# A convolution moved to channels on the partitions, and its logits from eight matmul tiles to four

## The chip, the cores and the metric

The kernel runs on one core of a Trainium2 chip. The metric is the device time of one execution in microseconds (us). The kernel before took 1312.17 us, the median of three runs (1308.29 to 1316.62).

## The reference

A depthwise causal convolution over 8 sequences of 3584 tokens with 192 channels comes first; the 7 taps are a softmax per head, and a head is 24 neighbouring channels. Then each token goes to one of 8 experts. The chosen expert can be inherited from the token before, so routing is a scan along the sequence.

```python
# convolution: x (8, 3584, 192), weight (8 heads, 7 taps)
w = softmax(weight, axis=-1)
out[b, s, h*24:(h+1)*24] = sum(w[h, k] * x_pad[b, s + k, h*24:(h+1)*24] for k in range(7))
# mixture of experts on that output, called x again
logits = x @ w_gate                      # (8, 3584, 8)
local_gate = sigmoid(x @ w_local)
for b in range(B):
    prev_e = -1
    for s in range(S):
        fresh_e = argmax(logits[b, s])
        e = fresh_e if s == 0 or local_gate[b, s] < 0.5 else prev_e
        prev_e = e
        p = softmax(logits[b, s])
        out[b, s] = p[e] * (relu(x[b, s] @ w1[e]) @ w2[e])     # w1: 192x1024, w2: 1024x192
```

All numbers are float32.

## The kernel before, in words

The 28672 tokens form 16 groups of 1792 (14 tokens on each of 128 partitions). Groups 0 and 1 take another way, with the convolution on TensorE (`wide`), and the change touches little of it. Each of the groups 2 to 15 goes through the following steps.

1. `conv` (L402): the window of x, 20 rows of 192 channels per partition, lies in `x_sb` with tokens on the partitions. For each of the 8 heads ScalarE writes the first tap (L413, 128x336 elements in 14 runs of 24) and VectorE adds the six others (L423), 48 VectorE instructions a group. The result is written straight into the group's token rows `y_sb`, which also hold the gate's factor and the token number.
2. `logits` (L601): VectorE turns the rows in 32x32 blocks into `z` (L606, four instructions), so that channels lie on the partitions, with four sets of 32 partitions for four sets of tokens. TensorE multiplies z by the gate's weights (L620): per block of 32 channels four column places times two row halves of 64 partitions. ScalarE copies the result out of PSUM (L625), VectorE turns it back (L628), and 16 small copies per group (L642 on ScalarE or L644 on VectorE) put it in order.
3. `route` (L650): argmax, the scan of inherited experts, and each token's place in its expert's list, some fifty small VectorE instructions; then tables of full units (`table`).
4. `put` (L821): GpSimd scatters the rows, 128 tokens at a time, into `slots` in DRAM, 14 times a group (L828).

Experts work on blocks of 128-token units of one expert, in this order: 28 single blocks, 43 pair blocks, then 23 blocks of four and a tail. A single or pair block is: rows loaded (L978), turned by TensorE (L394), hidden layer (L1047), relu on ScalarE (L1056), output layer (L1068), scaling of one half of the sum on ScalarE (L1078), and of the other, added to it, on VectorE (L1082), which frees the PSUM of the product, then a scatter into the output (L1096). Blocks of four multiply with seven products in place of eight (`seven`, L1211 to L1246; L1217 is the copy of its first product) and end with L1261, L1271 and L1276.

The order of instructions is written out by the program itself; each engine works through its own queue in that order. Between the parts of a block `step(time)` (L1322) emits side work, convolution and routing, until costs of `time` are used up. The costs are numbers that the generators yield: 0.6 for a tap, 0.2 for most small instructions. A pair block has steps of 4.8, 1.2 and 3.6, a single block 2.1, 1.2 and 1.3, a block of four the four of `SIDE`. A step runs until its time is zero or less; outside the blocks of four what it overshoots is forgotten. Routing comes first where it can run; at "pe" it waits for a step with room in PSUM, at "hop" it yields to convolution for the rest of the step.

Four pools of one buffer (`ys`) hold the token rows of four, later three groups; `yt` holds z. Convolution of group g starts only when the scatters of group g - 3 have been emitted and routing of group g - 2 has begun (L1297). From the last pair blocks on, the fourth pool holds the rows of blocks of four.

The softmaxed taps `c` are made at the start on one partition and spread to all by a matmul that also spreads the sums' reciprocals `rz` (L211 to L216). `rz` and the exponentials `hank` serve groups 0 and 1.

Of the kernel before, what the change touches and what calls it, by code (L numbers as in the profile page):

```python
# [8 lines left out]
F32 = mybir.dt.float32  # L9
# [86 lines left out]
TQ = (NT + 3) // 4  # L96
WA = F * KD // 2
# [14 lines left out]
def kernel(  # L112
# [4 lines left out]
    weight: bass.AP,  # L117
    wh: bass.AP,
# [28 lines left out]
    def load_x(g):  # L147
        x_sb = xs.tile([P, NX, D], F32, name="x_sb")
        src = x[g // PER]
        win = bass.AP(tensor=src.tensor, offset=src.offset + g % PER * PT * D,  # L150
                      ap=[[NT * D, P], [1, NX * D]])
        nc.sync.dma_start(out=x_sb.rearrange("p t d -> p (t d)"), in_=win)
        return x_sb
# [14 lines left out]
    c = cst.tile([P, H, KC], F32, name="c")  # L168
    nm = cst.tile([P, H], F32, name="nm")
    rz = cst.tile([P, H], F32, name="rz")  # L170
    with tc.tile_pool(name="scr", bufs=1) as scr:
# [6 lines left out]
        nc.sync.dma_start(out=wg, in_=wgl)  # L178
        x_in[1] = load_b(1)
# [13 lines left out]
        wide_w = scr.tile([P, 2 * H + H * KC], F32, name="wide_w")  # L193
# [9 lines left out]
        wc = ws[:, H:].rearrange("o (h k) -> o h k", k=KC)  # L203
# [7 lines left out]
        nc.vector.tensor_tensor(wc, w, bcast(ws[:, :H], KC), op=Alu.mult)  # L211
        cps = hps_p.tile([P, 512], F32, name="hps")
        nc.tensor.matmul(cps[:, :H + H * KC], lhsT=ones, rhs=wide_w[:, H:], start=True, stop=True)
        awake(2)
        nc.vector.tensor_copy(rz, cps[:, :H])
        nc.vector.tensor_copy(c.rearrange("p h k -> p (h k)"), cps[:, H:H + H * KC])  # L216
    wgb, wgq = wg[:, :3, :], wg[:, 3:, :]

# [179 lines left out]
    def row_tile(g):  # L398
        at = g % 4 if g < NARROW else (g + 1) % 3
        return ys[at].tile([P, NB, DG], F32, name="y_sb")  # L400

    def conv(g, x_sb):  # L402
        y_sb = row_tile(g)[:, :NT, :]
        got[g] = y_sb

        def cols(h):
            return y_sb[:, :, Y0 + h * GS:Y0 + (h + 1) * GS]

        def chans(h, k):
            return x_sb[:, k:k + NT, h * GS:(h + 1) * GS]  # L410

        def first(h):
            nc.scalar.activation(cols(h), chans(h, 0), Act.Copy, scale=c[:, h, 0:1])  # L413

        first(0)
        yield 0
        for h in range(H):
            if h + 1 < H:
                first(h + 1)
            if h == H // 2 and 2 < g < NPART - 1:  # L420
                x_in[g + 1] = load_x(g + 1)
            for k in range(1, KC):
                nc.vector.scalar_tensor_tensor(cols(h), chans(h, k), c[:, h, k:k + 1],  # L423
                                               cols(h), Alu.mult, Alu.add)
                yield 0.6
# [175 lines left out]
    def logits(g, y_sb):  # L601

        z = z_tile()[:, :NT * D].rearrange("p (t d) -> p t d", d=D)
        for t in range(0, NT, TQ):
            u = min(t + TQ, NT)
            nc.vector.transpose(z[:, t:u, :], y_sb[:, t:u, Y0:Y0 + D])  # L606
            yield 0.2 * (u - t)
        yield "pe"


        if late_p:
            both = st["bank"].tile([P, 2, 512], F32, name="ps")
            lps = [both[:, half, :TQ * Q] for half in range(2)]
        else:
            lps = [hps_p.tile([P, TQ * Q], F32, name="hps") for half in range(2)]
        begin = [min(TQ * j, NT - TQ) for j in range(4)]
        for b in range(DQ):
            for j in range(4):
                for half, rows in halves():
                    nc.tensor.matmul(lps[half][Q * j:Q * j + Q, :], lhsT=wgq[rows, b, :],  # L620
                                     rhs=z[rows, begin[j]:begin[j] + TQ, b * Q:(b + 1) * Q],
                                     start=(b == 0), stop=(b == DQ - 1))
# [4 lines left out]
        lq = sm.tile([P, 2 * TQ, Q], F32, name="lq", bufs=1)  # L627
        nc.vector.transpose(lq.rearrange("p t e -> p (t e)"), ls.rearrange("p h x -> p (h x)"))  # L628
        yield 0.4
        lt = sm.tile([P, NT + 2, E + 1], F32, name="lt")  # L630
# [3 lines left out]
        for r in range(4):  # L634
            for j in range(4):
                t, u = TQ * j, min(TQ * (j + 1), NT)
                at = r // 2 * TQ + t - begin[j]
                e0 = r % 2 * (E + 1)
                dst = lt[Q * r:Q * r + Q, t:u, :]
                src = lq[Q * j:Q * j + Q, at:at + u - t, e0:e0 + E + 1]  # L640
                if aside:
                    nc.scalar.copy(dst, src)  # L642
                else:
                    nc.vector.tensor_copy(dst, src)  # L644
                    yield 0.12
            if aside:
                yield "hop"
        return lt

    def route(g):  # L650
        y_sb = got.pop(g)
        lt = yield from logits(g, y_sb)
        lg = lt[:, :NT, :E]
# [15 lines left out]
        nc.vector.tensor_scalar(fr, lt[:, :NT, E], 0.0, None, Alu.is_lt)  # L669
# [579 lines left out]
    def output_late(n, wb, xg, hT, rows_next=None, between=None):  # L1249

        for part, h in enumerate(hT):
# [35 lines left out]
    LEAD = 2  # L1287
# [3 lines left out]
          "due": False, "hot": False, "since": 0, "bank": None, "over": 0}  # L1291

    def start_conv():
        g = st["conv"] + 1

        free = not any(p[0] <= g - 3 for p in to_put)
# [303 lines left out]
```

## Time and profile before

| what | value |
|---|---|
| median of three runs | 1312.17 us |
| profiled execution: time, span | 1309.78 us, 1308.1 us |
| mean granted TensorE clock | 0.998 |
| TensorE, VectorE, ScalarE, GpSimd busy | 98%, 73%, 47%, 42% of the span |
| taps on VectorE (L423) | 672, 384.5 us |
| logits on TensorE (L620) | 1344 matmul records, 25.0 us |

The profile is of one execution. A row of a group gives the line, engine, operation, tiles and shapes, the count, then busy time and the mean duration in ns, then the engine's idle time ahead of it and what ended it. A matmul of float32 numbers shows as two records. A row of the order of time begins with start and length in us and can hold several instructions (x16); idle time before it and its releaser stand in brackets. PE is TensorE, PEld its weight loads, DVE VectorE, ACT ScalarE, POOL GpSimd; ends of matmuls are modelled, so a busy TensorE can hide small gaps.

### The profile page before, as it was taken

How to read it: one execution, taken by the hardware profiler on the slowest of the kernel's cores; microseconds unless marked ns; L12 is line 12 of the kernel's file. 1: busy time of each engine (PE TensorE's matmuls, PEld its weight loads, DVE VectorE, ACT ScalarE, POOL GpSimd, SP SyncE). 2: the span in 40 equal slices, each digit the busy share in tenths (PEclk: the TensorE clock that was granted, in tenths of full speed). 3: DMA queues.
4: the chain of work that ended last, by engine and by line, in shares of the span. 5: the costliest groups of instructions: out<-in, count | busy, mean ns of one | idle time of the engine just before them, and what ended most of it. 6: DMA issues, size and time to landing. Idle time of an engine off the chain costs nothing. (4 is left out here: it accounts for less than half of the span.)

```text
span 1308.1 us, 39979 instructions
## 1 busy us (share of the span) xinstructions
PE 1276.2 (98%) x15750; PEld 1206.7 (92%) x15750; DVE 956.1 (73%) x2602; ACT 617.5 (47%) x1407; POOL 553.1 (42%) x619
## 2 busy tenths in 40 slices
PE   9899999999999999999999999999999999999997
PEld 7798999999999999899999899999999899999996
DVE  5888898889888788788988998898857844431111
ACT  5345555445555645456463454454434434342332
POOL 4444443534344444444435633654462664421211
PEclk9999999999999999999999999999999999999999
DMA  5789988857767767667696655555455637536894
GB/s 197 272 342 387 373 345 347 296 201 270 259 213 263 257 219 259 215 231 259 206 282 174 181 163 154 149 150 151 125 171 113 194 108 189 155 95 193 268 326 156
DMA packets 130243, 291.18 MB, mean 223 GB/s; under 512 B 87936, under 2 KB 104759, under 8 KB 114306
## 3 DMA queue, kind: packets, MB, share of 16 engines
q1 hardware_dynamic: 107728, 243.35, 56.6%
q0 software_dynamic: 22320, 45.22, 10.2%
q8 instruction: 126, 2.06, 0.7%
q14 instruction: 67, 0.55, 0.1%
q10 hardware_dynamic: 2, 0.00, 0.0%
HBM read 242.92 MB, written 46.07 MB: 221 GB/s over the span
## 5 line engine op out<-in xcount | busy, mean ns | idle before, releaser
L423 DVE SCALAR_TENSOR_TENSOR y_sb<-x_sb,c,y_sb 128x336 f32<-128x336 f32 x672 | 384.5, 581 | 33.3 <-ACT y_sb L413 11.0
L1068 PE MATMUL yps<-wb,hT 64*128 64x192 f32 x3648 | 318.6, 326 | 5.2 <-ACT hT L1056 3.0
L1047 PE MATMUL hps<-xT,wb 64*128 64x256 f32 (+1 forms) x3408 | 315.4, 336 | 2.6 <-issue 1.3
L828 POOL DMA_INDIRECT slots<-y_sb,posi x228 | 227.9, 1000 | 208.9 <-PE yps L1068 150.3
L1261 PE MATMUL ps<-wb,hot 64*128 64x192 f32 x3680 | 309.7, 324 | 2.1 <-issue 1.8
L1261 PEld LDWEIGHTS ps<-wb,hot 64*128 64x128 f32 x3680 | 299.3, 187 | 9.4 <-ACT hot L1235 5.0
L1068 PEld LDWEIGHTS yps<-wb,hT 64*128 64x128 f32 x3648 | 297.4, 187 | 10.2 <-ACT hT L1056 5.1
L1047 PEld LDWEIGHTS hps<-xT,wb 64*128 64x128 f32 x3408 | 283.2, 187 | 23.6 <-issue 3.6
L1096 POOL DMA_INDIRECT out_dram<-o_sb,head x115 | 120.6, 1049 | 296.7 <-DVE o_sb L1276 270.9
L1056 ACT ACTIVATE hT<-hps 128x512 f32<-128x512 f32 (+1 forms) x284 | 130.4, 510 | 161.0 <-PE hps L1047 116.5
L1096 POOL DMA_INDIRECT out_dram<-o_sb,xg x114 | 117.1, 1028 | 207.8 <-DVE o_sb L1082 112.4
L1271 ACT ACTIVATE o_sb<-ps,head 128x192 f32<-128x192 f32 x115 | 43.0, 418 | 205.2 <-PE ps L1261 178.9
L1276 DVE SCALAR_TENSOR_TENSOR o_sb<-ps,head,o_sb 128x192 f32<-128x192 f32 x115 | 43.2, 411 | 111.2 <-ACT o_sb L1271 108.6
L1029 ACT COPY xT<-xps 64x256 f32<-64x256 f32 (+4 forms) x284 | 105.1, 370 | 9.5 <-PE yps L1068 2.2
L1078 ACT ACTIVATE o_sb<-yps,xg 128x192 f32<-128x192 f32 x114 | 43.3, 418 | 125.2 <-PE yps L1068 96.9
L1135 DVE STREAM_TRANSPOSE xT<-y_sb 128x768 f32<-128x768 f32 (+1 forms) x65 | 54.8, 870 | 61.7 <-PE ps L1156 31.2
L1211 PE MATMUL ps<-xT,wb 64*128 64x256 f32 x736 | 88.5, 377 | 1.0 <-DVE xT L1187 1.0
L1211 PEld LDWEIGHTS ps<-xT,wb 64*128 64x128 f32 x736 | 75.3, 187 | 4.9 <-issue 2.2
L1082 DVE SCALAR_TENSOR_TENSOR o_sb<-yps,xg,o_sb 128x192 f32<-128x192 f32 x114 | 43.4, 412 | 33.1 <-ACT o_sb L1078 27.5
L1235 ACT ACTIVATE hot<-hot 128x512 f32<-128x512 f32 x46 | 26.4, 622 | 83.6 <-DVE hot L1233 61.1
L1156 PE MATMUL ps<-xT,wb 64*128 64x128 f32 (+1 forms) x912 | 64.5, 294 | 0.5 <-DVE xT L1135 0.5
L1156 PEld LDWEIGHTS ps<-xT,wb 64*128 64x128 f32 x912 | 62.6, 188 | 1.2 <-DVE xT L1135 1.1
(281 smaller groups left out, 1337.8 us busy)
## 6 DMA issues: line engine op xcount, KB each, us to landing
wb<-in_w_dram SPq DMA_DIRECT2D x109, 1536.0 KB
x_sb<-in_x_dram SPq DMA_DIRECT2D x14, 1920.0 KB
y_sb<-slots SPq DMA_DIRECT2D x92, 192.0 KB
xg<-slots SPq DMA_DIRECT2D x43, 195.0 KB
wb<-in_w_dram SPq DMA_DIRECT2D x12, 512.0 KB
slots<-y_sb,posi POOLq DMA_INDIRECT x228
x_sb<-in_xb_dram SPq DMA_DIRECT2D x4, 768.0 KB
y_sb<-slots SPq DMA_DIRECT2D x60, 48.0 KB
```

The lines of the kernel that those rows point to most:

```text
L423: nc.vector.scalar_tensor_tensor(cols(h), chans(h, k), c[:, h, k:k + 1], cols(h), Alu.mult, Alu.add)
L828: ins = nc.gpsimd.indirect_dma_start(out=slots[:, :], in_=rows, in_offset=None, out_offset=bass.IndirectOffsetOnAxis(ap=to, axis=0)).ins
L1029: copied = nc.scalar.copy(a, b)
L1047: ins = nc.tensor.matmul(hps[half][:, j, w], lhsT=wb[rows, f0:f0 + P], rhs=xT[rows, d, w], start=(d == 0 and j == 0), stop=(d == KD - 1), ...
L1056: nc.scalar.activation(hT[:, m:m + 2, w], hps[half][:, :, w], Act.Relu)
L1068: ins = nc.tensor.matmul(yps[half][:, k * D:(k + 1) * D], lhsT=hT[rows, m, k * P:(k + 1) * P], rhs=wb[rows, WA + m * D:WA + (m + 1) * D], ...
L1082: nc.vector.scalar_tensor_tensor(o_sb[:, k, :], y[k][1], xg[:, k, 0:1], o_sb[:, k, :], Alu.mult, Alu.add)
L1096: sent = nc.gpsimd.indirect_dma_start(out=out, in_=o, in_offset=None, out_offset=bass.IndirectOffsetOnAxis(ap=xg.bitcast(I32)[:, k, 1:2], ...
L1135: nc.vector.transpose(xT.rearrange("p d (j t) -> p j d t", t=Q)[:, js], rows[:, js].rearrange("p j (d t) -> p j d t", t=Q))
L1156: nc.tensor.matmul(hps[:, half, j, :], lhsT=wb[rows, f0:f0 + P], rhs=xT[rows, d, :], start=(d == 0 and j == 0), stop=(d == KD - 1), skip_g ...
L1211: ins = nc.tensor.matmul(to[:, half, j, :], lhsT=b[rows, j * P:(j + 1) * P], rhs=a[rows, :], start=(first and j == 0), stop=True, skip_gro ...
L1261: ins = nc.tensor.matmul(yps[:, half, k * D:(k + 1) * D], lhsT=h[two][rows, side, j, k * P:(k + 1) * P], rhs=wb[rows, f * D:(f + 1) * D], ...
```

## The change

- x arrives rearranged by the host: channels of a block of 32 on the partitions, four sets of tokens, 20*32 numbers a channel block (`_part_layout`). A window still is one load of 15360 bytes per partition.
- `conv` works on z directly: per group 6 blocks of 32 channels instead of 8 heads, each one first tap on ScalarE and six on VectorE over 448 numbers in a row. Groups with even numbers write z in the third `ys` buffer, odd ones in `yt`.
- The taps are now one number per partition, block and tap: loaded spread out (`taps`) and softmaxed on all partitions by `taps_begun` and `taps_done`, six small VectorE steps and an exponential at the start. The old path for `c` goes, that for `rz` stays.
- `logits` begins with the matmuls: per block of 32 channels 2 column places times 2 row halves over 224 columns, so that half 0 fills output partitions 0 to 63 and half 1 those from 64. Then VectorE turns z into rows, with the same number of 32x32 blocks (cost 0.24 per token row, 0.2 before). 8 small copies take the place of 16, and one "hop" goes.
- A tap costs 0.68 in the plan, 0.6 before. Steps and `SIDE` stay.
- Token rows have three buffers for groups under 8, two after. Routing of group g starts only when the scatters of g - 3 (later g - 2) are emitted; convolution of group g needs the rows of group g - 2 turned.

```diff
     def row_tile(g):
-        at = g % 4 if g < NARROW else (g + 1) % 3
-        return ys[at].tile([P, NB, DG], F32, name="y_sb")
+        return ys[(0, 1, 3)[g % 3] if g < NARROW else g % 2].tile([P, NB, DG], F32, name="y_sb")
+    def rows_free(g):
+        return not any(p[0] <= (g - 3 if g < NARROW else g - 2) for p in to_put)
...
     def conv(g, x_sb):
...
+        z = (z_tile() if g % 2 else
+             ys[2].tile([P, NB, DG], F32, name="y_sb").rearrange("p b d -> p (b d)"))
+        z = z[:, :NT * D].rearrange("p (b s) -> p b s", b=DQ)
+        def chans(b, k):
+            return x_sb[:, b, k * Q:(k + NT) * Q]
+        def first(b):
+            nc.scalar.activation(z[:, b, :], chans(b, 0), Act.Copy, scale=c[:, b, 0:1])
...
-                nc.vector.scalar_tensor_tensor(cols(h), chans(h, k), c[:, h, k:k + 1],
-                                               cols(h), Alu.mult, Alu.add)
-                yield 0.6
+                nc.vector.scalar_tensor_tensor(z[:, b, :], chans(b, k), c[:, b, k:k + 1],
+                                               z[:, b, :], Alu.mult, Alu.add)
+                yield 0.68
...
     def logits(g, z):
+        yield "pe"
...
         for b in range(DQ):
-            for j in range(4):
+            for j in range(2):
                 for half, rows in halves():
-                    nc.tensor.matmul(lps[half][Q * j:Q * j + Q, :], lhsT=wgq[rows, b, :],
-                                     rhs=z[rows, begin[j]:begin[j] + TQ, b * Q:(b + 1) * Q],
+                    at = DR * half + Q * j
+                    nc.tensor.matmul(lps[half][at:at + Q, :], lhsT=wgq[rows, b, :],
+                                     rhs=z[rows, b, j * TH * Q:(j + 1) * TH * Q],
                                      start=(b == 0), stop=(b == DQ - 1))
-        ls = sm.tile([P, 2, TQ * Q], F32, name="ls", bufs=1)
-        for half in range(2):
-            nc.scalar.copy(ls[:, half, :], lps[half])
-        yield "hop"
+        ls = sm.tile([P, TH * Q], F32, name="ls", bufs=1)
+        for half, rows in halves():
+            nc.scalar.copy(ls[rows], lps[half][rows])
+        y_sb = row_tile(g)[:, :NT, :]
+        zt = z.rearrange("p b (t s) -> p t b s", s=Q)
         for t in range(0, NT, TQ):
             u = min(t + TQ, NT)
+            nc.vector.transpose(y_sb[:, t:u, Y0:Y0 + D].rearrange("p t (b s) -> p t b s", s=Q),
+                                zt[:, t:u])
+            yield 0.24 * (u - t)
+        st["turned"] = g
...
+    def taps_begun():
+        nc.vector.tensor_reduce(cz, c, axis=AX.X, op=Alu.max)
+        nc.vector.tensor_tensor(c, c, bcast(cz, KC), op=Alu.subtract)
+        nc.scalar.activation(c, c, Act.Exp)
+    def taps_done():
+        nc.vector.tensor_reduce(cz, c, axis=AX.X, op=Alu.add)
+        nc.vector.tensor_scalar(cz, cz, 1e-9, None, Alu.add)
+        nc.vector.reciprocal(cz, cz)
+        nc.vector.tensor_tensor(c, c, bcast(cz, KC), op=Alu.mult)
...
-        free = not any(p[0] <= g - 3 for p in to_put)
-        if (st["cgen"] is None and g < NPART and g <= st["route"] + LEAD and free
+        if (st["cgen"] is None and g < NPART and g <= st["turned"] + 2
...
-        if st["rgen"] is None and st["route"] < done:
+        if st["rgen"] is None and st["route"] < done and rows_free(st["route"] + 1):
```

More of the change, by code (lines that the diff above doesn't have):

```diff
@@ L96 @@
 TQ = (NT + 3) // 4
+TH = NT // 2
 WA = F * KD // 2
@@ L117 @@
     weight: bass.AP,
+    taps: bass.AP,
     wh: bass.AP,
@@ L147, in load_x @@
     def load_x(g):
[L148 to L153, printed above, removed]
+        x_sb = xs.tile([P, NX, D], F32, name="x_sb").rearrange("p t d -> p (t d)")
+        nc.sync.dma_start(out=x_sb, in_=x[g])
+        return x_sb.rearrange("p (b s) -> p b s", b=DQ)
     def load_b(g):
@@ L178 @@
         nc.sync.dma_start(out=wg, in_=wgl)
+        nc.sync.dma_start(out=c, in_=taps)
         x_in[1] = load_b(1)
@@ L599, in gathered, with logits @@
         return xg
[L601 to L607, printed above, removed]
+    def logits(g, z):
         yield "pe"
@@ L644, in logits @@
                     nc.vector.tensor_copy(dst, src)
-                    yield 0.12
+                    yield 0.16
             if aside:
                 yield "hop"
-        return lt
+        return y_sb, lt
     def route(g):
-        y_sb = got.pop(g)
-        lt = yield from logits(g, y_sb)
-        lg = lt[:, :NT, :E]
+        y_sb, lt = yield from logits(g, got.pop(g))
+        lg = lt[:, :, :E]
         mx = sm.tile([P, NT], F32, name="mx")
@@ L1560, in _block_layout, with _part_layout, _channel_taps @@
     return xb
+def _part_layout(np, x):
+    at = (PT * np.arange(PER)[:, None, None] + NT * np.arange(P)[:, None] + np.arange(NX))
+    v = x[:, at].reshape(NPART, 4, Q, NX, DQ, Q)
+    return v.transpose(0, 1, 5, 4, 3, 2).reshape(NPART, P, DQ * NX * Q)
+def _channel_taps(np, w):
+    heads = (Q * np.arange(DQ) + np.arange(P)[:, None] % Q) // GS
+    return w[heads]
 def _tap_layout(np, w):
```

59 lines of the change are left out of this document (26 added, 33 removed).

## The prediction

> **What bounds the kernel now.** I read the page's busy shares and slices first, then the mean per stage, then one ordinary block in order of time, then the groups of the lines that the diff touches.
>
> ```profile
> PE 1276.2 (98%) x15750; PEld 1206.7 (92%) x15750; DVE 956.1 (73%) x2602; ACT 617.5 (47%) x1407; POOL 553.1 (42%) x619
> PE   9899999999999999999999999999999999999997
> DVE  5888898889888788788988998898857844431111
> PEclk9999999999999999999999999999999999999999
> ```
>
> TensorE is busy nearly everywhere at full clock; VectorE is close behind until about slice 31, where convolution and routing end. The stages (columns: window, its length, then busy time per engine):
>
> ```profile
> 54.70:214.20 159.50, 153.11 (x2475) 147.19 (x2474) 138.88 (x412) 86.67 (x268) 69.43 (x70) 1.00 0.92 354
> 214.20:697.00 482.80, 481.39 (x6024) 455.27 (x6022) 411.80 (x1228) 258.10 (x643) 205.55 (x201) 1.00 0.72 247
> 697.00:1037.00 340.00, 332.10 (x3748) 309.02 (x3746) 283.23 (x675) 151.79 (x251) 166.35 (x177) 1.00 0.55 152
> ```
>
> These are the single blocks (128 tokens), the pair blocks (256) and the blocks of four with side work. TensorE shows 6.4, 1.4 and 7.9 us of idle time there: 15.7 us is about all that a faster VectorE could give back, plus bubbles that the modelled ends hide. Two pair blocks of the middle stage on TensorE, the second with a group's logits (L620) in it:
>
> ```profile
> 306.81 5.35 PE L1047 MATMUL hps<-xT,wb 64*128 64x256 f32 x48
> 311.99 0.40 PE L394 MATMUL xps<-ident,xg 64*128 64x64 f32 x8
> 312.22 5.42 PE L1068 MATMUL yps<-wb,hT 64*128 64x192 f32 x64
> 317.47 5.35 PE L1047 MATMUL hps<-xT,wb 64*128 64x256 f32 x48
> 322.65 0.40 PE L394 MATMUL xps<-ident,xg 64*128 64x64 f32 x8
> 322.98 1.59 PE L620 MATMUL hps<-z,wg 64*32 64x128 f32 x96
> 329.81 5.35 PE L1047 MATMUL hps<-xT,wb 64*128 64x256 f32 x48
> ```
>
> The plain block takes 317.47 - 306.81 = 10.66 us. Two tiles of 64 rows run side by side, so it streams 48*256/2 + 64*192/2 = 12,288 columns and 8*64 = 512 of the transposes: 12,800 columns in 10.66 us, 0.833 ns a column, with nothing left over. The block with logits takes 12.34 us, so logits cost 1.68 us of undivided TensorE time. The middle stage is bound by TensorE's streaming and by nothing else.
>
> **The change part by part.** First the logits, which lie on the path.
>
> ```profile
> L620 PE MATMUL hps<-z,wg 64*32 64x128 f32 x1056 | 20.2, 273 | 2.2 <-issue 2.2
> L620 PE MATMUL ps<-z,wg 64*32 64x128 f32 x288 | 4.8, 272 | 0.0
> L280 PE MATMUL yps<-z,wg 128*32 128x224 f32 x32 | 1.9, 352 | 0.0
> ```
>
> There are (1056 + 288)/96 = 14 groups, three of them in blocks of four. A group now issues 96 records of 128 columns, eight tiles at a time (4 column places, 2 row halves): 12 rounds. Their starts spread over 1.59 - 0.27 = 1.32 us, 0.11 us a round, which is what 128 columns at 0.833 ns cost (0.107): the eight tiles do overlap fully. The new code issues 48 records of 224 columns, and half 0 writes only column places 0 and 1, half 1 only 2 and 3: four tiles at a time, again 12 rounds, each 224*0.833 = 0.187 us. L280 shows such rounds: 32 records in two runs of 0.95 us, of which 0.352 is the last record, so 0.6 us for three steps, 0.2 a round. A group then costs 12*(0.187 - 0.107) = 0.96 us more, and 14 groups 13.4 us: half the array stands idle while fewer instructions run. [...]
>
> Next VectorE's taps and what surrounds them.
>
> ```profile
> L423 DVE SCALAR_TENSOR_TENSOR y_sb<-x_sb,c,y_sb x672: 490/571/1541, 42.6 to 942.4; 128x336 f32<-128x336 f32 x168
> L662 DVE SCALAR_TENSOR_TENSOR eq<-ex,ed 128x112 f32<-128x112 f32 x14 | 4.7, 334 | 0.5
> L1187 DVE TENSOR_TENSOR xT<-xT 128x256 f32<-128x256 f32 x23 | 9.8, 425 | 0.8
> L606 DVE STREAM_TRANSPOSE z<-y_sb 128x768 f32<-128x768 f32 x42 | 38.3, 953 | 0.4
> L644 DVE COPY lt<-lq 32x36 f32<-32x36 f32 x60 | 11.2, 187 | 0.9
> ```
>
> From 112 to 336 elements this instruction grows from 334 to 571 ns, 1.06 ns an element, so the runs of 24 elements cost nothing visible and 448 elements take 571 + 118 = 0.69 us. Bounds: 0.63 us (the plain two-input form, 425 ns at 256, carried on at 1.06) and 0.76 (571 scaled by 448/336). I take 0.69, the same operation. 504 of them are 348 us against 672*0.571 = 384: 36 us less on VectorE. The transposes are the same 768 elements in the other direction; I charge nothing. The small copies go from 16 to 8 a group: 16*0.20 = 3.2 us becomes 8*0.23 = 1.8 where VectorE makes them (12 of a group's 16 have that width: 60/12 = 5 groups), and the rest leave ScalarE, which at 47% nobody waits for; so do 28 of 112 first taps.
> [...]
>
> What does that buy? The plan hands out side work by its own cost units, 0.6 a tap before, 0.68 after, and its budgets per block are not changed. In a pair block 4.8 + 1.2 + 3.6 gives 8 + 2 + 6 = 16 taps either way.
>
> ```profile
> 297.50 0.74 DVE L1082 SCALAR_TENSOR_TENSOR o_sb<-yps,xg,o_sb 128x192 f32<-128x192 f32 x2
> 298.15 9.48 DVE L423 SCALAR_TENSOR_TENSOR y_sb<-x_sb,c,y_sb 128x336 f32<-128x336 f32 x16
> 307.55 0.73 DVE L1082 SCALAR_TENSOR_TENSOR o_sb<-yps,xg,o_sb 128x192 f32<-128x192 f32 x2
> 318.13 0.74 DVE L1082 SCALAR_TENSOR_TENSOR o_sb<-yps,xg,o_sb 128x192 f32<-128x192 f32 x2 [1.69 <-ACT o_sb L1078]
> ```
>
> Such a block costs VectorE 307.55 - 297.50 = 10.05 us now, 0.6 under TensorE's 10.66, and 10.05 + 16*0.118 = 11.94 after, 1.28 over. At most 36/16 = 2.25 of them follow each other, so VectorE falls 2.9 us behind. Its cover: L1082 frees the product's PSUM at 308.28 and the next product (L1068) starts at 312.22, 3.9 us later. That hides it nearly always; I add 0.5 us.
> Per group the plan's units fall from 28.8 + 18.8 (the yields of routing and tables) = 47.6 to about 43.9, from 5 pair blocks to 4.6 at 9.6 units; scatters, three a pair block and 14 a group, hold it at 4.7. So side work ends sooner, and no time is won in the middle.
>
> One wait changes its place. Token rows are now written by VectorE's transposes at routing, no longer by ScalarE's first tap, so a transpose waits for the scatters of the rows two groups before, and taps and L1082 queue behind it.
>
> ```profile
> 302.92 0.96 POOL L828 DMA_INDIRECT slots<-y_sb,posi  x1 [0.84 <-PE yps L1068]
> 304.19 0.96 POOL L828 DMA_INDIRECT slots<-y_sb,posi  x1 [0.30 <-issue]
> ```
>
> The plan starts routing only when those scatters are issued; one takes 0.96 us on GpSimd's queue. If each routing met the last of them it would cost 14*1 us; I take zero, since it falls into the same 3.9 us of cover. Likewise logits no longer wait for transposes, but none waits now.
>
> Single blocks: 2.1 + 1.2 + 1.3 gives 9 taps before and 4 + 2 + 2 = 8 after.
>
> ```profile
> 0.00:54.70 54.70, 5.59 (x11) 1.00 0.64 225
> 54.70:214.20 159.50, 78.50 (x141) 1.00 0.92 354
> 697.00:1308.00 611.00, 70.14 (x112) 1.00 0.58 169
> ```
>
> ```profile
> 65.87 5.34 DVE L423 SCALAR_TENSOR_TENSOR y_sb<-x_sb,c,y_sb 128x336 f32<-128x336 f32 x9
> 66.01 2.70 PE L1068 MATMUL yps<-wb,hT 64*128 64x192 f32 x29 [1.10 <-DVE o_sb L1082]
> 71.46 5.28 DVE L423 SCALAR_TENSOR_TENSOR y_sb<-x_sb,c,y_sb 128x336 f32<-128x336 f32 x9
> ```
>
> (The first fence is the taps alone in three stages, the last column all DMA in GB/s.) Here VectorE binds: 71.46 - 65.87 = 5.59 us a block against (48*128/2 + 32*192/2 + 4*64)*0.833 = 5.33 on TensorE. Nine taps start (5.28 - 0.571)/8 = 0.589 us apart, 5.30, so 0.29 is L1082. After: 8*(0.589 + 0.118) + 0.29 = 5.95 us. With 141/9 = 15.7 such blocks before and 106/8 = 13.2 after, the excess goes from 4.1 to 8.2 us, +4.1; the smaller copies give 3*1.4 = 4.2 back. Call it zero, and let 1.5 us of the three logits here vanish in TensorE's 6.4 us of waiting: -1.5.
>
> Late taps: six small VectorE steps join the start, where VectorE's chain is never idle but once.
>
> ```profile
> 39.70 0.26 DVE L474 COPY nf<-hps 16x112 f32<-16x112 f32 x1 [1.41 <-remote]
> L888 DVE TENSOR_REDUCE sums<-add 128x3 f32<-128x24 f32 x19 | 3.4, 178 | 0.7
> ```
>
> At about 0.2 us each, the last four fall into that 1.41 us; the first two cost 0.4, and the step of 2.4 units, still four taps, 4*0.118 more: +0.8 us (bounds 0 and 1.7). The new load of taps, 128x42 numbers ahead of the second half-megabyte tile, is 21.5 KB in a queue that moves 225 GB/s then: 0.1 us, and I leave it out.
>
> Blocks of four:
>
> ```profile
> 696.94 1.01 ACT L1217 COPY hot<-ps 128x1024 f32<-128x1024 f32 x1 [0.20 <-PE ps L1211]
> 1036.93 1.01 ACT L1217 COPY hot<-ps 128x1024 f32<-128x1024 f32 x1 [0.18 <-PE ps L1211]
> 1158.23 1.01 ACT L1217 COPY hot<-ps 128x1024 f32<-128x1024 f32 x1 [0.18 <-PE ps L1211]
> ```
>
> One L1217 opens each of 23 blocks. The last six take 121.30/6 = 20.22 us; the 16 with side work 339.99/16 = 21.25, 16.5 us more in all: 3*1.68 = 5.0 of logits and 11.5 of VectorE delays, 0.7 a block. Side work left at 697 is 112*0.6 + 3*18.8 = 124 units in 16 blocks, 7.7 a block. The saving of 14*3.7 = 52 units, less some 9 that the scatters hold back, leaves 81, 10 or 11 blocks. Five blocks fewer at 0.7 give -3.7; larger taps in the others cost +0.7: -3.0.
>
> Sum: 13.4 + 0.5 - 1.5 + 0.8 - 3.0 = +10.2 us. The profiled execution took 1309.78 us (span 1308.1), so 1320.0; it lies 2.4 us under the median of 1312.17, and I carry that over: 1322.
>
> **The rivals.** *VectorE becomes the bound in the middle.* Its lag passes the 3.9 us of cover when conv blocks and routing blocks add up; then the 410*0.75/16 = 19 conv blocks cost up to 1.28 us each, 24 us. For it: VectorE is already at 411.80 of 482.80 us; against: each logits block gives it 2.6 us to recover. Half of it gives 1334. Chance 0.22.
> *VectorE's relief wins: faster.* If the plan running ahead takes away all VectorE waits (6.4 + 1.4 + 11.5 = 19.3 us and as much of the bubbles as brings 27), the time is 1312 + 13.4 - 27 = 1299. It needs taps at 0.63 us or less, so that a pair's 16 stay near 10.66 us a block. Against it: the waits come from long runs of taps ahead of L1082, and those runs grow. Chance 0.10, with half relief (1311) another 0.10.
> *The four tiles do not overlap across column places.* Then 24 rounds, 2.2 us more a group, 1322 + 31 = 1353. L280 and the eight-fold overlap of L620 speak against it: 0.03.
>
> **How the numbers follow.** The forecast has 0.55, its own range 1313 to 1331. About 1% (13 us) is what a measurement of this kernel can tell from no change: 1299 to 1325. A third of the forecast's case lies above 1325. Slower: 0.18 + 0.22 + 0.03 = 0.43. Faster: 0.09. The rest, 0.48, is same. The range 1305 to 1334 leaves out the full relief, half of the VectorE rival, and the serial tiles.
>
> **What would show it.** The logits' run should grow from 1.59 to about 2.5 us, and a pair block with logits from 12.34 to 13.3; plain pair blocks stay at 10.66. Taps should number 504 at 0.69 us. Waits of L1068 on L1082 beyond single blocks would show the first rival. The side work should end before the eleventh block of four. The forecast is wrong if plain pair blocks lengthen, or if blocks of four with side work come down to 20.2 us.

## The result, and the profile after

The changed kernel took 1328.43 us (median of four runs, 1327.47 to 1331.32) against 1312.58 us of the kernel before beside it (1308.29 to 1316.62): a ratio of 1.0125, 95% interval [1.0089, 1.0161]. The profiled execution took 1327.47 us, span 1325.8; before 1309.78 and 1308.1. So 17.7 us of span have to be found. One execution of the changed kernel, in the second group of experiments below, ran at a granted clock of 0.65 and took 1909 us; no median or ratio here counts it.

The page of the changed kernel, busy shares and VectorE's slices:

```profile
PE 1290.5 (97%) x15078; PEld 1209.3 (91%) x15078; DVE 902.7 (68%) x2398; ACT 602.1 (45%) x1308; POOL 558.3 (42%) x619
DVE  6788889898797897888988986677444444341111
```

VectorE has 53 us less to do (956.1 us before) and is done with side work some slices sooner. The kernel takes longer all the same. Busy time by stage shows where. Columns: window, its length, then PE, PEld, DVE, ACT, POOL busy with counts, granted clock, DMA share, GB/s. The windows end at the first hidden layer, at the first pair block, and at the first and last start of a block of four (L1217, after L1227). Before:

```profile
0.00:45.80 45.80, 40.74 (x282) 35.59 (x283) 30.45 (x109) 22.52 (x59) 19.80 (x73) 1.00 0.65 225
45.80:219.82 174.02, 165.46 (x2645) 158.62 (x2646) 151.94 (x467) 92.32 (x284) 75.80 (x77) 1.00 0.90 344
219.82:696.94 477.12, 475.71 (x5935) 449.59 (x5934) 406.78 (x1206) 254.07 (x632) 204.57 (x200) 1.00 0.72 247
696.94:1158.23 461.29, 453.39 (x5044) 424.34 (x5042) 339.53 (x774) 202.48 (x322) 224.02 (x240) 1.00 0.54 150
1158.23:1308.10 149.87, 140.91 (x1856) 138.59 (x1852) 27.38 (x51) 46.14 (x111) 28.94 (x30) 0.99 0.70 225
```

After:

```profile
0.00:51.66 51.66, 42.97 (x282) 36.89 (x282) 30.71 (x112) 22.83 (x59) 20.08 (x73) 0.90 0.66 228
51.66:228.84 177.18, 168.43 (x2501) 161.11 (x2500) 151.78 (x459) 90.50 (x277) 81.76 (x81) 0.99 0.88 333
228.84:718.07 489.23, 485.90 (x5600) 448.45 (x5600) 421.57 (x1203) 250.73 (x580) 219.30 (x213) 1.00 0.71 247
718.07:1174.67 456.60, 451.93 (x4848) 424.28 (x4847) 271.25 (x578) 191.96 (x283) 208.22 (x225) 1.00 0.53 144
1174.67:1325.80 151.13, 141.22 (x1856) 138.53 (x1852) 27.40 (x51) 46.09 (x111) 28.96 (x30) 0.98 0.70 223
```

The differences are +5.9 at the start, +3.2 in the single blocks, +12.1 in the pair blocks, -4.7 in the blocks of four, +1.3 in the tail. The start is the surprise: its granted clock is 0.90, and I had expected 0.8 us there.

The taps are as predicted:

```profile
L435 DVE SCALAR_TENSOR_TENSOR y_sb<-x_sb,c,y_sb 128x448 f32<-128x448 f32 x252 | 171.0, 689 | 33.4 <-ACT y_sb L425 16.6
L435 DVE SCALAR_TENSOR_TENSOR z<-x_sb,c,z 128x448 f32<-128x448 f32 x252 | 173.8, 699 | 26.5 <-ACT z L425 11.7
```

TensorE over pair blocks of the changed kernel, in order of time, with a group's logits (L625):

```profile
295.66 5.35 PE L1057 MATMUL hps<-xT,wb 64*128 64x256 f32 x48
...
306.42 2.47 PE L625 MATMUL hps<-y_sb,wg 64*32 64x224 f32 x48
308.83 5.45 PE L1057 MATMUL hps<-xT,wb 64*128 64x256 f32 x48
...
315.19 5.47 PE L1078 MATMUL yps<-wb,hT 64*128 64x192 f32 x64 [0.68 <-ACT hT L1066]
320.50 5.35 PE L1057 MATMUL hps<-xT,wb 64*128 64x256 f32 x48
```

The block with logits takes 308.83 - 295.66 = 13.17 us (12.34 before). But the block behind it takes 320.50 - 308.83 = 11.67 in place of 10.66, with a wait for ScalarE's relu ahead of its output layer. Four blocks of the stage look like this one. The waits of TensorE in the whole pair stage (engine, tile and line, what ended the wait, then us in total, times, and the longest) show nothing else but one of 0.2 us at its end:

```profile
PE yps L1078 <- ACT hT L1066: 2.7, 4, 0.7
```

### The profile page after: what moved, and what is told of

Its sections match the earlier page's. It is cut to its first block, busy times and chain, and to the rows that moved or that the text cites. A ratio compares the mean times of both kernels' runs of the same rounds, so it can differ in the third digit from the quotient of the medians.

```text
span 1325.8 us, 38317 instructions
## 1 busy us (share of the span) xinstructions
PE 1290.5 (97%) x15078; PEld 1209.3 (91%) x15078; DVE 902.7 (68%) x2398; ACT 602.1 (45%) x1308; POOL 558.3 (42%) x619
## 4 chain that ended last, share of the span: by engine, by line
PE 87%; DVE 7%; issue 2%; DMA 2%; ACT 1%; SPq 1%; POOL 0%; POOLq 0%; DVEq 0%; ACTq 0%
PE yps L1078 21%; PE hps L1057 21%; PE ps L1271 21%; PE ps L1221 13%; PE ps L1166 4%; PE xps L1221 3%; DVE y_sb L435 2%; PE hps L625 2%; DMA wb<-in_w_dram 1%; PE xps L403 1%; DVE z L435 1%; PE hps L253 1%; DVE xT L1145 0%; DMA y_sb<-slots 0%; PE hps L190 0%
## 5 line engine op out<-in xcount | busy, mean ns | idle before, releaser
L838 POOL DMA_INDIRECT slots<-y_sb,posi x228 | 233.4, 1024 | 189.5 <-PE yps L1078 113.3
L1078 PEld LDWEIGHTS yps<-wb,hT 64*128 64x128 f32 x3648 | 299.1, 188 | 10.2 <-ACT hT L1066 4.4
L1066 ACT ACTIVATE hT<-hps 128x512 f32<-128x512 f32 (+1 forms) x284 | 130.1, 511 | 158.9 <-PE hps L1057 134.0
L435 DVE SCALAR_TENSOR_TENSOR y_sb<-x_sb,c,y_sb 128x448 f32<-128x448 f32 x252 | 171.0, 689 | 33.4 <-ACT y_sb L425 16.6
L435 DVE SCALAR_TENSOR_TENSOR z<-x_sb,c,z 128x448 f32<-128x448 f32 x252 | 173.8, 699 | 26.5 <-ACT z L425 11.7
L1286 DVE SCALAR_TENSOR_TENSOR o_sb<-ps,head,o_sb 128x192 f32<-128x192 f32 x115 | 43.3, 413 | 149.2 <-ACT o_sb L1281 141.3
L1039 ACT COPY xT<-xps 64x256 f32<-64x256 f32 (+4 forms) x284 | 105.1, 370 | 11.4 <-PE yps L1078 4.5
L1241 DVE TENSOR_TENSOR hot<-ps,hot 128x1024 f32<-128x1024 f32 x23 | 28.2, 1225 | 75.3 <-PE ps L1221 71.5
L1221 PEld LDWEIGHTS ps<-xT,wb 64*128 64x128 f32 x736 | 75.8, 187 | 3.9 <-issue 1.4
```

The source lines that it names most:

```text
L435: nc.vector.scalar_tensor_tensor(z[:, b, :], chans(b, k), c[:, b, k:k + 1], z[:, b, :], Alu.mult, Alu.add)
L838: ins = nc.gpsimd.indirect_dma_start(out=slots[:, :], in_=rows, in_offset=None, out_offset=bass.IndirectOffsetOnAxis(ap=to, axis=0)).ins
L1039: copied = nc.scalar.copy(a, b)
L1066: nc.scalar.activation(hT[:, m:m + 2, w], hps[half][:, :, w], Act.Relu)
L1078: ins = nc.tensor.matmul(yps[half][:, k * D:(k + 1) * D], lhsT=hT[rows, m, k * P:(k + 1) * P], rhs=wb[rows, WA + m * D:WA + (m + 1) * D], ...
L1221: ins = nc.tensor.matmul(to[:, half, j, :], lhsT=b[rows, j * P:(j + 1) * P], rhs=a[rows, :], start=(first and j == 0), stop=True, skip_gro ...
```

## The start: an exponential in ScalarE's queue

ScalarE at the start of the changed kernel:

```profile
25.21 0.97 ACT L278 COPY z<-hps 128x448 f32<-128x448 f32 x2
33.20 0.24 ACT L220 ACTIVATE c<-c 128x42 f32<-128x42 f32 x1 [7.02 <-DVE c L219]
33.34 0.95 ACT L278 COPY z<-hps 128x448 f32<-128x448 f32 x2
```

VectorE, at the end of the work on the first group's tables:

```profile
32.74 0.19 DVE L218 TENSOR_REDUCE cz<-c 128x6 f32<-128x42 f32 x1
32.96 0.20 DVE L219 TENSOR_TENSOR c<-c,cz 128x42 f32<-128x42 f32 x1
```

TensorE there:

```profile
26.65 0.95 PE L284 MATMUL yps<-z,wg 128*32 128x448 f32 x6
33.91 0.96 PE L284 MATMUL yps<-z,wg 128*32 128x448 f32 x1 [6.30 <-issue]
...
37.03 2.91 PE L604 MATMUL yps<-y_sb,hot 112*128 112x195 f32 x8
```

TensorE before:

```profile
30.22 1.60 PE L592 MATMUL yps<-y_sb,hot 112*128 112x195 f32 x8 [1.15 <-DVE hot L586]
```

The first part of the late softmax, `taps_begun`, is emitted ahead of the rest of the second sequence's convolution. Its exponential (L220) goes into ScalarE's queue, waits 7.0 us for two VectorE steps (L218, L219) that stand behind the first group's tables and start only at 32.74, and holds two copies (L278) behind it that depend on neither. TensorE needs those copies and stands idle for 6.3 us. Then it runs at a granted clock of 0.50, until about 39.8. TensorE's row calls the wait "issue", so the reason has to be read from ScalarE's rows. The windows of the changed kernel (columns as above):

```profile
28.00:30.00 2.00, 0.00 (x0) 0.00 (x0) 1.86 (x7) 0.00 (x0) 1.40 (x3) 0.88 0.15 44
30.00:32.00 2.00, 0.00 (x0) 0.00 (x0) 1.93 (x7) 0.00 (x0) 1.70 (x2) 0.50 0.29 87
36.00:38.00 2.00, 2.00 (x7) 1.14 (x5) 0.00 (x0) 0.53 (x1) 0.00 (x0) 0.50 0.91 213
38.00:40.00 2.00, 2.00 (x10) 1.91 (x8) 0.00 (x0) 0.00 (x0) 0.00 (x0) 0.56 0.95 350
40.00:42.00 2.00, 2.00 (x15) 2.00 (x14) 1.45 (x8) 0.00 (x0) 0.94 (x1) 1.00 1.05 424
```

Eight products of L604 take 2.91 us, against 1.60 before, at a granted clock of 1.00 (window 30 to 32).

## The experiments

They were run in three groups. Chips differ by more than one per cent: the kernel before took 1291.31 us in the first group, 1308.30 in the second and 1291.41 in the third (the first and third ran on the same chip). So medians and stages are compared within a chip. The ratios are estimates with a 95% interval and need not equal the quotient of two medians. The stages come from one execution of each kernel, and executions of one kernel lie up to 10 us apart (1312.56 to 1322.51 us for "exponential later, hop"), so small differences of one stage say little on their own. The stages of all profiled executions, cut as above (us; in brackets the groups of logits in the blocks of four):

| kernel | start | singles | pairs | fours | tail | median | ratio to before |
|---|---|---|---|---|---|---|---|
| group 1: exponential later | 44.19 | 169.39 | 487.30 | 450.96 (2) | 151.86 | 1305.37 | 1.0101 [1.0077, 1.0124] |
| eight tiles | 51.92 | 171.21 | 484.33 | 450.00 (2) | 151.13 | 1310.09 | 1.0137 [1.0117, 1.0157] |
| hop | 50.35 | 170.29 | 482.86 | 452.38 (2) | 153.62 | 1309.88 | 1.0130 [1.0109, 1.0150] |
| before with late taps | 51.51 | 169.18 | 473.71 | 454.15 (3) | 149.75 | 1300.77 | 1.0068 [1.0049, 1.0087] |
| group 2: changed, again | 50.94 | 175.58 | 488.71 | 454.39 (2) | 151.48 | 1326.78 | 1.0150 [1.0104, 1.0196] |
| before, again | 45.78 | 173.39 | 476.61 | 459.70 (3) | 149.21 | 1306.38 (one run) | |
| exponential later, hop | 45.65 | 177.86 | 485.07 | 455.91 (2) | 154.31 | 1315.11 | 1.0060 [1.0039, 1.0081] |
| exponential later, hop, eight tiles | 46.64 | 176.49 | 481.69 | 455.28 (2) | 152.40 | 1312.89 | 1.0033 [1.0016, 1.0051] |
| group 3: the same, again | 46.02 | 170.80 | 475.79 | 450.71 (2) | 152.88 | 1295.06 | 1.0028 [1.0012, 1.0043] |
| the same, tap counted at 0.72 | 45.39 | 176.33 | 475.00 | 451.66 (2) | 152.43 | 1300.37 | 1.0068 [1.0049, 1.0087] |
| the same, tap counted at 0.78 | 44.63 | 174.78 | 475.74 | 452.20 (2) | 152.45 | 1302.22 | 1.0087 [1.0057, 1.0117] |
| changed, with filling products | 48.90 | 169.90 | 487.31 | 451.23 (2) | 148.55 | 1307.62 (one run) | |

**The exponential behind the convolution.** The edit to the changed kernel:

```diff
     def taps_begun():
...
         nc.vector.tensor_tensor(c, c, bcast(cz, KC), op=Alu.subtract)
-        nc.scalar.activation(c, c, Act.Exp)
...
     rest(wide1)
+    nc.scalar.activation(c, c, Act.Exp)
```

> The changed kernel with one instruction moved: ScalarE's exponential of the taps (L220) stands behind the second sequence's last steps instead of ahead of them; the two VectorE steps stay. Theory A: in the changed kernel this exponential held ScalarE's queue for 7.0 us (it waits for VectorE), the copies of z behind it held TensorE's L284 for 6.3 us, and the first hidden layer started at 51.66 us instead of 45.80. Then it starts near 46 us again and the time falls by about 5.9 us, from 1328.4 to 1322.5. Theory B: the wait that the row calls issue comes from the added load of the taps or from fetching instructions. Then nothing changes: 1328.

ScalarE, then TensorE:

```profile
33.07 0.24 ACT L1422 ACTIVATE c<-c 128x42 f32<-128x42 f32 x1 [4.18 <-DVE c L219]
```

```profile
27.30 0.94 PE L288 MATMUL yps<-z,wg 128*32 128x224 f32 x16
29.39 1.59 PE L603 MATMUL yps<-y_sb,hot 112*128 112x195 f32 x8 [1.15 <-DVE hot L597]
```

The exponential runs at the same time as in the changed kernel and still waits, but nothing of urgency stands behind it. The eight products take 1.59 us again, and the first hidden layer starts at 44.19 us, 6 to 8 us sooner than in the two other kernels of its group that keep the late taps' order. On the chip of the second group, where both were profiled, the start with the line moved and the hop put back is 45.65 us, beside 45.78 of the kernel before and 50.94 of the changed kernel: one line's place is the whole delay. In the whole time the ratio fell to 1.0101, from 1.0125 and 1.0150 of the changed kernel, with intervals that overlap; the stage shows it better.

**The kernel before with late taps alone.** The same softmax steps at the same places, on a tile that nothing reads, with one small load for it:

```diff
+    c2 = cst.tile([P, DQ, KC], F32, name="c2")
...
     rest(route0)
+    taps_begun()
...
     hots(1)
+    taps_done()
```

> The kernel before with the late taps alone, on a tile that nothing reads: the added load, the two VectorE steps and ScalarE's exponential after the first sequence's routing, the four last steps at their place. Convolution, logits and the old taps stay as before. Theory A (ScalarE's queue): the start grows by about 5.9 us, 1312.6 to 1318.5, with the same idle stretch of L275. Theory B (it comes from the new layout, or from the lighter start without the old taps): under 1.5 us, the six small steps alone.

TensorE in it, and a window:

```profile
34.71 0.95 PE L290 MATMUL yps<-z,wg 128*32 128x448 f32 x1 [6.30 <-ACT z L284]
```

```profile
32.00:34.00 2.00, 0.00 (x0) 0.00 (x0) 1.76 (x12) 0.00 (x0) 1.65 (x2) 0.50 0.29 87
```

The first hidden layer moves from 45.8 to 51.5 us with no other part of the change there. Here the row names the copy of ScalarE. The granted clock falls to 0.50 here too. The whole is 9.5 us slower than before. Some 3 to 4 us beyond the start are not placed, since no profile of the kernel before was taken on that chip.

**Filling TensorE's idle time.** The changed kernel with products into an unused bank during the wait:

```diff
         yield from turned(1, range(3))
+        if g:
+            fill = hps_p.tile([P, 512], F32, name="hps")
+            for _ in range(28):
+                nc.tensor.matmul(fill[:, :P], lhsT=ones, rhs=ones, start=True, stop=True)
         products()
```

> The changed kernel with 28 further products of 128 columns into an unused bank ahead of the second sequence's products, in the 6 us in which TensorE stands idle there. If the idle time lowers the granted clock (0.50 for some 9 us after it in the changed kernel), the clock stays near 1.0 and the first hidden layer starts 2 to 3 us earlier, at 48 to 49 us in place of 51 to 52; the other 3 to 4 us of the delay are the idle time itself and stay. If the clock is lowered by something else, 0.50 stays and the start stays at 51 to 52 us.

TensorE, then two windows:

```profile
26.60 6.43 PE L307 MATMUL hps<-ones 128*128 128x128 f32 x56
...
48.90 1.27 PE L1061 MATMUL hps<-xT,wb 64*128 64x128 f32 x18
```

```profile
30.00:32.00 2.00, 2.00 (x21) 2.00 (x20) 1.93 (x7) 0.00 (x0) 1.66 (x2) 1.00 0.30 87
36.00:38.00 2.00, 2.00 (x16) 1.97 (x15) 0.32 (x2) 0.27 (x1) 0.00 (x0) 1.00 0.99 305
```

The clock stays at 1.00, and the first hidden layer starts at 48.90: 1.5 and 3.0 us sooner than in the two kernels of the same chip with the unfilled wait (50.35 and 51.92), and 4.7 later than with the exponential moved. So here idle time is what lowered the clock (0.50 with 6.3 us of it, 1.00 with it filled), and of a delay of 6 to 8 us the clock of 0.50 is 1.5 to 3; the rest is the wait itself.

**The hop put back.** `yield "hop"` ends routing's share of the current step, so that what follows is emitted in a later step. The change had dropped the one behind the logits. The run puts a pause ahead of the small copies, a little later than the dropped one stood (ahead of VectorE's transpose of the logits). Without it the copies that put the logits in order (L653) come ahead of the next block's relus in ScalarE's queue. In the changed kernel, ScalarE in the block that starts at 308.83:

```profile
308.95 0.70 ACT L630 COPY ls<-hps 64x224 f32<-64x224 f32 x2 [1.69 <-PE hps L625]
314.02 0.50 ACT L653 COPY lt<-lq 32x63 f32<-32x63 f32 x2 [4.36 <-DVE lq L640]
314.54 2.07 ACT L1066 ACTIVATE hT<-hps 128x512 f32<-128x512 f32 x4
```

The copies wait 4.36 us for VectorE's transpose L640, which stands behind taps and four transposes of z into rows (L635); the four relus come all at once, after the hidden layer's end. The groups of these copies, before and after, show it as well:

```profile
L642 ACT COPY lt<-lq 32x36 f32<-32x36 f32 (+1 forms) x144 | 31.0, 215 | 3.4 <-DVE lq L628 1.5
```

```profile
L653 ACT COPY lt<-lq 32x63 f32<-32x63 f32 x72 | 17.5, 243 | 18.4 <-DVE lq L640 17.5
```

```diff
-        if aside and late_p:
+        if aside:
             yield "hop"
```

> The changed kernel with one pause of routing put back: the small copies of logits on ScalarE begin one step later in the pair blocks too. Theory A: in the pair blocks after some of the logits, ScalarE's copy L653 waits 4.4 us for VectorE's L640, the relu behind it comes late and TensorE waits; those four or five blocks of 11.67 us come down to 10.67, about 4 us less, 1324. Theory B: these blocks are long since VectorE is busy 12.1 us in them; then they stay at 11.67, 1328.

ScalarE in the block behind the logits, which starts at 300.40:

```profile
303.35 1.09 ACT L1066 ACTIVATE hT<-hps 128x512 f32<-128x512 f32 x2 [2.13 <-PE hps L1057]
305.88 1.09 ACT L1066 ACTIVATE hT<-hps 128x512 f32<-128x512 f32 x2 [1.44 <-PE hps L1057]
...
308.51 0.50 ACT L653 COPY lt<-lq 32x63 f32<-32x63 f32 x2
```

Relus follow their products again, the copies wait for nothing, and no block of 11.67 us is left. TensorE waits for no relu in the pair stage of this run; with only the exponential moved it is 2.7 us in four waits, as in the changed kernel. The pair stage is 4.4 us shorter than with only the exponential moved (482.86 against 487.30), about four such blocks. The whole time does not show the gain: the ratio is 1.0130. In this execution the tail is 153.62 us, the second longest of the table, and TensorE waits 3.7 us there for VectorE's transposes of rows from `slots`, where it waits 0.9 in the changed kernel.

**Eight tiles again.** Channel-wise convolution stays; logits go back to 32 rows by 128 columns in four column places times two row halves, with 16 copies:

```diff
-            for j in range(2):
+            for j in range(4):
                 for half, rows in halves():
-                    at = DR * half + Q * j
-                    nc.tensor.matmul(lps[half][at:at + Q, :], lhsT=wgq[rows, b, :],
-                                     rhs=z[rows, b, j * TH * Q:(j + 1) * TH * Q],
+                    nc.tensor.matmul(lps[half][Q * j:Q * j + Q, :], lhsT=wgq[rows, b, :],
+                                     rhs=z[rows, b, begin[j] * Q:(begin[j] + TQ) * Q],
```

> The changed kernel with the logits in eight tiles over 128 columns again (four column places, two row halves; the last two token rows of a place are computed twice as before), with 16 small copies at half the plan's cost each, so that the plan hardly moves. Theory A: TensorE streams columns and 12 rounds of 224 cost 14*0.84 = 11.8 us more than 12 of 128: 1328.4 - 11.8 = 1316.6, and a pair block with logits takes 12.3 us, not 13.17. Theory B: VectorE, with 16 larger taps in a block, has become the bound of the pair blocks; then less than 5 us comes back, 1324 or more.

ScalarE, then TensorE, behind a group's logits:

```profile
307.40 0.90 ACT L654 COPY lt<-lq 32x36 f32<-32x36 f32 x4 [4.94 <-DVE lq L640]
```

```profile
301.93 5.45 PE L1058 MATMUL hps<-xT,wb 64*128 64x256 f32 x48
308.84 5.47 PE L1079 MATMUL yps<-wb,hT 64*128 64x192 f32 x64 [1.23 <-ACT hT L1067]
314.14 5.35 PE L1058 MATMUL hps<-xT,wb 64*128 64x256 f32 x48
```

Six of nine logits blocks fell from 13.17 to 12.28 or 12.29 us, as expected. But twice as many copies now wait ahead of the relus: four in this block, and it takes 314.14 - 301.93 = 12.21 us in place of 11.67; the three others of its kind take 12.85. TensorE's waits for the relu in the pair stage grew from 2.7 to 6.8 us:

```profile
PE yps L1079 <- ACT hT L1067: 6.8, 4, 1.9
```

The pair stage is 3.0 us shorter than with only the exponential moved (484.33 against 487.30), where nine groups would have given 8.0. Of the expected 12 us little came: the ratio is 1.0137, beside 1.0125 and 1.0150 of the changed kernel, both where the kernel before took 1308 us or more. The two terms are not independent: tiles can only be judged once the hop is back.

**Both repairs of ScalarE's queue, then eight tiles too, beside both kernels.**

> The changed kernel once more, without an edit, on the same chip as the three below, so that they can be compared stage by stage. The chip of the first four runs was faster in the single blocks and in the blocks of four than that of the first pair of profiles, with the same instructions. Theory A and B alike: about 16 us over the kernel before, of which the start (first hidden layer at 51.7 us in place of 45.8) is 6 and the pair blocks 12.

> The kernel before once more, without an edit, for its stages on the same chip. Theory A and B alike: the first hidden layer at 45.8 us, pair blocks 473 to 477 us; single blocks and blocks of four may differ from the first profile by several us, as the chip does.

> The changed kernel with both repairs of ScalarE's queue: the exponential of the taps moved behind the second sequence, and the pause ahead of the small copies. Logits stay in four tiles. Theory A: the two gains add: 7.5 us at the start (e1 showed 44.2 instead of 51.7) and 4.5 in the pair blocks, so about 12 us under the changed kernel of this call, 4 us over the kernel before. The first hidden layer starts near 44.2 us, no pair block of 11.67 us is left. Theory B (VectorE's larger taps bind): the pair blocks stay where they are, only the start is won, 7 us.

> As the one above, and the logits in eight tiles over 128 columns: only the new convolution with its transposes and buffers is left of the change. Theory A: 14 groups at 0.84 to 0.89 us less of TensorE, 12 us under the run above and 6 to 8 us under the kernel before, which would beat both; the 16 small copies on ScalarE may give back up to 4. Theory B: VectorE binds, and the logits' time is taken up by its lag: within 3 us of the run above.

The changed kernel again was 1.5% slower than before. The two repairs took 11.7 us off (1326.78 to 1315.11), as expected. In the stages the start is 5.3 us shorter and the pair blocks 3.6; the other three are longer by 6.6 in all, but the one profiled execution, 1320.63 us, was the second slowest of its ten, and that of the changed kernel its fastest. The eight tiles took off only 2.2 us more, where 12 had been expected, though seven of nine logits blocks were again 0.7 to 0.9 us shorter. In that execution one pair block took 14.27 us and five others 0.3 to 1.2 us too much, so I suspected that the plan, which counts a tap at 0.68 us where it takes 0.69 to 0.70, overfills VectorE.

**Dearer taps in the plan.** The same kernel once more, and with

```diff
-                yield 0.68
+                yield 0.72
```

or 0.78.

> The changed kernel with both repairs of ScalarE's queue and eight tiles of 32 rows by 128 columns, once more, as the mark for the other two of this group. The saving from tiles was 0.9 us in each of 14 blocks on their own (12.3 against 13.2 us) and only 2 us in the whole. Both theories expect 1.003 of the kernel before.

> The same, and the planner counts a tap at 0.72 us in place of 0.68 (it takes 0.69 to 0.70). Theory A: the planner overfills VectorE by some 0.02 us a tap, the lag grows over a part's 48 taps and 14 other steps and is paid back in stalls; with a dearer tap the saving of the tiles comes through, 6 to 10 us less, about 0.997 of the kernel before. Theory B: the stalls are of waits for tiles and loads and not of VectorE's load; no change within 3 us.

> The same with a tap at 0.78 us. Theory A: the plain blocks get room of 1 us, stalls are gone from single blocks and pairs, but the convolutions end later and a group or two of logits comes in the blocks of four; total 5 to 10 us less than at 0.68. Theory B: no gain, and some us more in the blocks of four, where convolution steps are then left over.

Theory A falls. The pair stage takes 475.79, 475.00 and 475.74 us, so there was nothing to win there, and the single blocks became 4 to 6 us longer, not shorter. There TensorE waits for rows that are still being loaded from `slots`: 2.8 us in one wait with a tap at 0.68, 7.6 us in four at 0.78. With 0.72 it is

```profile
PE xps L402 <- DMA xg<-slots: 7.2, 4, 2.9
```

So the added time is mostly waits for these loads; why they come later was not tested. And on this chip the tiles' gain is there: 475.79 against 482.86 with the hop alone, 7.1 us where 9 groups of 0.89 make 8.0. One of its logits blocks on TensorE:

```profile
327.73 5.34 PE L1057 MATMUL hps<-xT,wb 64*128 64x256 f32 x48
...
338.49 1.59 PE L624 MATMUL hps<-z,wg 64*32 64x128 f32 x96
340.01 5.45 PE L1057 MATMUL hps<-xT,wb 64*128 64x256 f32 x48
```

That is 12.28 us, as before the change (12.34). Why the other chip showed only 2.2 us between the medians stays open. It was the best version found, still 0.28% [0.12, 0.43] slower than before, so no version beats the kernel before. Where these 3.6 us lie is not shown: beside the kernel before with late taps, the only form of it profiled on that chip, this version is 3.1 us longer in the tail, 2.1 in the pair blocks and 1.6 in the single blocks, and 3.4 shorter in the blocks of four, in one execution of each.

## Why the prediction was right or wrong

The forecast of 1322 us lay 6 us under the time, on the right side; its range of 1305 to 1334 held it. By the prediction's bound of 1% it is slower (0.43), if barely, and not the likelier "same" (0.48); the interval of the ratio holds 1% as well. The likeliest mechanism held, the longer rounds of the logits, with two costs beside it that the sum did not have. That the time still lay within the forecast's own range, 1313 to 1331, is partly luck: neither of the two is named among the prediction's terms or rivals, and the logits and the blocks of four came out cheaper than the sum had them. Its sum of +10.2 us stands against +17.7 in the profiled executions.

- **Late taps, +0.8: the step that failed.** The start grew by 5.9. The step priced "six small VectorE steps" and left out the seventh instruction that `taps_begun` issues, the exponential on ScalarE. At 0.24 us it costs nothing by itself. What it costs is its place: it carries VectorE's lateness, a wait of 7.0 us, into another queue, ahead of work that TensorE needs. Moving that one line, and adding those lines alone to the kernel before, show it from both sides.
- **"ScalarE, which at 47% nobody waits for": the same mistake a second time.** It is true of ScalarE's load and false of its order. The dropped hop costs 1.0 us in each of four pair blocks; putting it back gave 4.4. The pair stage's +0.5 was meant for VectorE's lag, which in fact stayed hidden: plain pair blocks other than these four stay at 10.67 us, and the wait that appeared is for L1066 (2.7 us), not L1092 (none in the pair stage). So the VectorE rival did not decide, and the sum's term for the middle was made up of the wrong thing.
- **Logits, +13.4: right, a little too large.** The run grew from 1.59 to 2.47 us and the block from 12.34 to 13.17, 0.83 us a group where 0.96 was predicted; 14 groups are 11.6 us, under the 13.4 of the sum. Twelve rounds in both forms fit the runs: less the last record the starts spread over 2.47 - 0.35 = 2.12 us, 0.18 a round, beside 0.11 before; at the 0.833 ns a column of a plain block (10.66 us for 12,800) 224 and 128 columns would be 0.187 and 0.107. The rival of 24 rounds, 2.2 us more a group, is out. Nine groups instead of eight fall into the pair stage, so 9*2.50 - 8*1.67 = 9.1 of its 12.1 us are logits.
- **Taps: right.** 504 of them at 0.69 to 0.70 us against 0.69, taken from the slope of two rows.
- **Early, -1.5 on top of three groups' logits:** found about +0.7 on top of them (3.2 - 2.5). TensorE's idle time there is 8.6 us before and 8.8 after, so none of the logits' time vanished in it. Which price of this term was off was not looked into.
- **Blocks of four, -3.0:** found -4.7, at two groups of logits in place of three. Over 22 periods of 20.22 us, before has 461.29 - 444.8 - 3*1.67 = 11.4 us of delays, after 456.60 - 444.8 - 2*2.5 = 6.8. Taps end at 821 us in place of 942, and side work before the eleventh block, as predicted. It is the only stage that became shorter with VectorE's 53 us less.
- **Transposes behind the scatters, put at nothing:** this held in the changed kernel, where they show no idle time ahead of them. In the two repaired kernels of the second group VectorE stands idle once ahead of them, for 4.3 and 4.8 us, and TensorE then waits 0.6 and 1.0 us in all for the scaling on VectorE (L1092), the only trace of the VectorE rival in the pair blocks; what ended the idle time the profile does not name.
- **Tail, not in the sum:** +1.3 here; 148.6 to 154.3 us in the variants of the changed kernel, against 149.9 and 149.2 in the two profiles of before. VectorE's transposes there wait for rows loaded from `slots`, in all 13.1 us before and 33.1 after, of which 0.5 and 0.9 us reach TensorE; what makes those loads later was not looked into.

## What to carry to other kernels

When a step is moved, list each of its instructions by engine and ask what stands behind each in that engine's queue; a 0.24 us instruction with a late input is as long as its wait for everything behind it (7.0 us here). A low busy share (ScalarE's 45% here) says that an engine has time, not that its order is free. And a scheduler's odd markers (a hop, a late exponential) may carry more than the arithmetic around them: with both put right and the tiles as before, what is left of the change, some 45 us less work for VectorE among it (910.6 us busy), still took 0.28% longer than the kernel before.

## What was not expected of the hardware

- In the changed kernel the granted clock fell to 0.50 about 2 us into TensorE's idle time: the last product ends at 26.65 + 0.95 = 27.6, and a mean of 0.88 in the window 28 to 30 puts the fall at 29.5, as an estimate with one step from 1.00 to 0.50. It came back at about 39.8 (0.56 in the window 38 to 40), nearly 6 us after work had begun again at 33.9. In the kernel before with late taps it fell 2.8 us into the idle time (the last product ends at 28.4, and a mean of 0.80 in the window 30 to 32 puts the fall at 31.2, the same estimate) and came back 3 to 4 us after work had begun again at 34.7 (0.50 in the window 36 to 38, 0.99 in 38 to 40). Filled with idle products, the same time showed 1.00 throughout. The two falls, 1.9 and 2.8 us into the idle time, are of one execution each.
- Chips differ: the kernel before took 1291 us on one and 1308 on another, and its single blocks 169.2 us (with late taps added) and 173.4 us.
- The same wait for a copy on ScalarE, 6.30 us of TensorE, was put down to "issue" in one trace (the changed kernel) and to the copy in another (the kernel before with late taps).
